# Padded heads straight from the projection for the first 512 tokens of a transformer block

## The chip, the cores and the metric

The kernel runs on one core of one Trainium2 chip. The core has five engines, each with its own instruction queue: TensorE (PE: matrix products from operands in SBUF, results into PSUM), VectorE (DVE), ScalarE (ACT), GpSimd (POOL) and SyncE (SP, which here issues every DMA). Engines run side by side and wait for one another on semaphores. Activations and weights lie in DRAM and are brought into SBUF, the on-chip memory with 128 partitions, by DMA.

The metric is the device time of one execution in microseconds, the median of the runs shown.

## The reference

One transformer block on 2048 tokens of width 640. A vector `c` gives six modulation vectors; a LayerNorm with scale and shift feeds sliding-window attention (32 heads of 20, each query sees itself and the 255 tokens before it), its output is projected, gated and added; a second LayerNorm feeds a gated MLP of width 1536, again gated and added.

```python
mod = (silu(c) @ w_mod).reshape(1, 6, 1, 640)
sa, ca, ga, sb, cb, gb = mod[:, 0..5]
h = layernorm(x) * (1 + ca) + sa
q, k, v = split(h @ wqkv)                      # 32 heads of 20
scores = q @ k.T * 20**-0.5                    # masked: 0 <= i - j < 256
x = x + ga * (softmax(scores) @ v) @ wo
h = layernorm(x) * (1 + cb) + sb
x = x + gb * ((sigmoid(h @ w_gate) * (h @ w_up)) @ w_down)
```

All inputs are bfloat16.

## The kernel before, in words

**Blocks, chunks and parts.** Tokens come in 16 blocks of 128. LayerNorm and the projections work on four chunks of four blocks (512 tokens). Attention, output projection and MLP work on five parts of 2, 2, 4, 4 and 4 blocks (`CHUNKS`, line 363). A part needs keys of its own blocks and of the two blocks before it, so the first two parts need chunk 0 alone, and the third (blocks 4 to 7) needs chunks 0 and 1.

**Order of the work.** The program lists operations with their reads and writes, an engine (or a choice of two), a planned duration, a priority and sometimes an earliest time (`tmin`). `schedule` (line 141) places them greedily: at each step it takes the engine whose next operation can start first, and among that engine's operations that can start at about the same time the one with the lowest priority number. The result is one fixed order for each engine, with buffers given out in that order; `emit` (line 274) writes it with semaphores. On the chip each engine works through its list in order and waits at each entry until its inputs are there, whatever lies behind it. That holds for SP too: a DMA whose source is not ready holds all DMAs behind it. Each DMA also waits for the one 24 places before it (`NDMA`).

**Opening.** `x` of chunk 0, a third of `w_mod` and the Q, K and V weights are loaded. GpSimd fills ten V buffers with ones (line 450) and two `Tn` buffers with zeros. PE runs warm-up matmuls on a V buffer (lines 500 to 509) until `w_mod` is there, and then the products for scale and shift (`scA`, `shA`, lines 568 and 570). `ln_stats` (line 574) computes mean and variance on VectorE and the reciprocal root on GpSimd for all four blocks of a chunk at once, then normalizes block by block (line 594). Chunk 0 is transposed on PE (line 629) and scaled on ScalarE or VectorE (line 634) into `hT`; later chunks are transposed by DMA (line 600).

**Q and K.** A score matmul needs head j of a group of four at partitions 32j to 32j+19, so heads of 20 have to be spread out to a stride of 32. `proj_qk` (line 654) makes five tiles of 128 features for Q and five for K, each a chain of five matmuls of 512 columns (line 513), copies each from PSUM into `stg` (line 648), stores it to DRAM (`dq`, `dk`), and reads it back into `QT` and `KT` by heads (line 674, four reads for each half of the heads). V needs no such round trip: `proj_v` (line 681) puts 20 columns of each head into a stride of 22, beside two columns of ones, which give the sums for the softmax.

**Attention.** For each group of four heads and each set of up to 512 key-query columns: scores on PE (four row tiles of the array at once, line 514), an exponential on ScalarE (line 755), masks on GpSimd (lines 771 and 773), the product with V on PE (line 514), and for each group transposes and the division on VectorE (`norm`, line 819). There is one PSUM buffer for scores. Parts 0 and 1 have 8 and 16 sets, the others 24 each. The result goes through DRAM (`doc`) to be transposed for the output projection. 

**MLP.** `outproj` (line 844) adds, normalizes and transposes into `h2T` (one buffer); `mlp` (line 868) makes gate and up (`wg`, `wu`, resident), tanh on ScalarE, the product on VectorE, and the down projection. PE takes scores (priority 10) and products with V (11) before projections (12 to 23), and the MLP last (40 and up), so projections and MLP fill the time in which scores wait for exponentials.

Of the kernel before, what the change touches and what calls it, by code (L numbers as in the profile page):

```python
# [344 lines left out]
def c_act(n):  # L345
    return 0.17 + n / 1200.0
# [19 lines left out]
def build(nc, A_x, A_wqkv, A_wo, B_x, B_w_gate, B_w_up, B_w_down, c, w_mod, out, S=2048):  # L366
# [17 lines left out]
    wg = sb("wg", [128, NDT, FF])  # L384
    wu = sb("wu", [128, NDT, FF])
# [14 lines left out]
    p_h2 = sbpool("h2T", 1, [128, NDT, 512])  # L400
# [18 lines left out]
    def R(name):  # L419
        return Res(name)  # L420

    R_wq, R_wk, R_wv, R_ident, R_ccol, R_cth, R_siluc, R_silubc = (
        R(n) for n in ("wq", "wk", "wv", "ident", "ccol", "cth", "siluc", "silubc"))
    R_wo = R("wo")
    R_wg = [R(f"wg{t}") for t in range(NDT)]
    R_wu = [R(f"wu{t}") for t in range(NDT)]
# [22 lines left out]
    for i in range(len(p_V.aps)):  # L449
        p_V.init[i].append(A("pool", lambda e, g, i=i: e.memset(p_V.aps[i][:], 1.0), 0.8, writes=[R("vi")], prio=1))  # L450
    for i in range(len(p_Tn.aps)):
        p_Tn.init[i].append(A("pool", lambda e, g, i=i: e.memset(p_Tn.aps[i][:], 0.0), 0.6, writes=[R("ti")], prio=2))
# [27 lines left out]
    for kt in range(NDT):  # L480
        dma(lambda kt=kt: wg[:, kt, :], lambda kt=kt: B_w_gate.rearrange("(t p) f -> p t f", p=128)[:, kt, :], 393216,
            writes=[R_wg[kt]], prio=30, tmin=27 + 1.6 * kt, tag="wg")
        dma(lambda kt=kt: wu[:, kt, :], lambda kt=kt: B_w_up.rearrange("(t p) f -> p t f", p=128)[:, kt, :], 393216,
            writes=[R_wu[kt]], prio=30, tmin=35 + 1.6 * kt, tag="wu")
    for q in range(4):
        dma(lambda q=q: wd[:, 3 * q:3 * q + 3, :],
            lambda q=q: B_w_down.rearrange("(t p) f -> p t f", p=128)[:, 3 * q:3 * q + 3, :], 491520,
            writes=[R_wd[q]], prio=30, tmin=43 + 2.0 * q, tag="wd")
# [17 lines left out]
    for i in range(9):  # L506
        o = A("pe", warm, 0.85, prio=90, extra=p_V.init[0] + wprev, tag="warm", writes=[R("w")])
        wprev = [o]
    p_S.init[0].extend(wprev)

# [63 lines left out]
    def ln_stats(blocks, src, dst, prio):  # L574
# [18 lines left out]
        for bi in range(n):  # L593
            A("dve", lambda e, g, bi=bi: e.tensor_scalar(dst[bi].ap[:], src[bi].ap[:], v(48 + 2 * bi, 1), v(60 + bi, 1),  # L594
                                                         op0=ALU.subtract, op1=ALU.mult), 0.56,
              reads=[src[bi].r(), st.r("r"), st.r(("m", bi))], writes=[dst[bi].r()], prio=prio - 0.5, tag="xh")
# [15 lines left out]
    def ln1(cc):  # L612
# [5 lines left out]
        ln_stats(blocks, src, src, 3 if cc == 0 else 16)  # L618
# [35 lines left out]
    def proj_qk(cc, mts, halves, prio):  # L654
        for which, (w, Rw) in enumerate(((wq, R_wq), (wk, R_wk))):
# [4 lines left out]
            for mt in mts:  # L660
                ps = Tile(p_M, f"{key}{cc}_{mt}")
                pairs = [(lambda kt=kt, mt=mt, w=w, ps=ps: (ps.ap[:], w[:, kt, mt * 128:(mt + 1) * 128],
                                                            hT[cc].ap[:, kt, :])) for kt in range(NDT)]
                s = Tile(p_stg, f"stg{key}{cc}_{mt}")
                pe_chain(ps, 512, pairs, [[Rw, hT[cc].r(kt)] for kt in range(NDT)], prio, f"proj{key}{cc}", hold=[s])
# [12 lines left out]

    dq = {}

    def proj_v(cc, prio):
        for bi in range(4):
            b = 4 * cc + bi
# [30 lines left out]
    def attention(a, i0, QB):  # L714
# [9 lines left out]
        for g in range(NG):  # L724
# [6 lines left out]
            for si, st in enumerate(sets):  # L731
# [17 lines left out]
                for (kb, q0, n) in st:  # L749
                    for j in range(4):  # L750
                        rd[KT[(kb // 4, hh)].r(j)] = 1
                        rd[qt.r(j)] = 1
# [115 lines left out]
    def mlp(a, i0, QB, x1, h2):  # L868
# [4 lines left out]
        for ft in range(NFT):  # L873
            pg, pu, sg = Tile(p_M, "g"), Tile(p_M, "u"), Tile(p_sig, "sig")
            for ps, w, Rw, tg in ((pg, wg, R_wg, "g"), (pu, wu, R_wu, "u")):
                pairs = [(lambda kt=kt, ft=ft, ps=ps, w=w: (ps.ap[:, 0:W], w[:, kt, ft * 128:(ft + 1) * 128],
                                                            h2.ap[:, kt, 0:W])) for kt in range(NDT)]
                last["m"] = [pe_chain(ps, W, pairs, [[Rw[kt], h2.r(kt)] for kt in range(NDT)], pr, f"mlp{tg}{a}",
                                      after=last["m"])]
# [30 lines left out]
    qkv(0)  # L910
    ln1(1)
# [71 lines left out]
```

## Time and profile before

| | us |
|---|---|
| median of 3 runs | 380.7 (377.94 to 381.37) |
| the profiled execution | 380.11 |
| its span, first to last instruction | 378.4 |
| mean granted TensorE clock | 0.954 of full speed |
| PE busy | 344.5 |
| ScalarE busy | 223.0 |
| VectorE busy | 218.8 |
| GpSimd busy | 177.0 |
| moved by DMA | 42.81 MB |

The profile is of one execution. Its times are microseconds from the start of the span, single instructions in nanoseconds where that is said. A row of the timeline gives start, duration, engine, line, operation, what is written and read, how many instructions are merged, and in brackets how long the engine had been idle and what ended that. A row of a group gives busy time, the mean nanoseconds of one instruction, and the idle time ahead of the group by what ended it. "SPq" is SP's queue at work on issuing a DMA; "PEclk" is the clock granted to TensorE as a share of full speed.

### The profile page before, as it was taken

Reading aid. Unit: us, or ns where it says so; the run is one execution under the profiler, and the core shown is the slowest. Engines: PE = TensorE matmul, PEld = TensorE weight load, DVE = VectorE, ACT = ScalarE, POOL = GpSimd, SP = SyncE. Lnnn points to the kernel's source line nnn. Section 1 sums busy time; section 2 is a strip of 40 time slices with the busy share of each in tenths; the row PEclk is TensorE's granted clock in tenths of the full one; section 3 lists DMA queues with packets and bytes.
Section 4 is the critical chain, followed back from the end, with each engine's and each line's share of the span. In section 5 each row is a group of like instructions: output and inputs, shape, how many; then the busy total and the mean of one; then the engine's idle time right before and its main releaser. Section 6 shows DMA issues by size and latency. Waiting matters only on the chain.

```text
span 378.4 us, 8381 instructions
## 1 busy us (share of the span) xinstructions
PE 344.5 (91%) x3198; PEld 172.9 (46%) x3198; DVE 218.8 (58%) x471; ACT 223.0 (59%) x207; POOL 177.0 (47%) x281
## 2 busy tenths in 40 slices
PE   5796697678999799999999879999999999989996
PEld 2453243123445244655556423353554345744464
DVE  4354175767877755556886545397564638433332
ACT  1352366776888769878888767878778421012210
POOL 8111144679676845666668574667567300000000
PEclk9999699579999889999999969999999999999999
DMA  6999799976365042034203511200343020320001
GB/s 215 338 303 192 232 309 373 291 195 197 95 149 144 17 126 75 29 94 101 89 19 88 112 47 36 88 2 20 45 114 87 2 87 3 74 66 0 0 19 52
DMA packets 52887, 42.81 MB, mean 113 GB/s; under 512 B 22768, under 2 KB 49648, under 8 KB 52848
## 3 DMA queue, kind: packets, MB, share of 16 engines
q1 hardware_dynamic: 52848, 42.29, 41.0%
q8 instruction: 25, 0.41, 0.4%
q14 instruction: 14, 0.11, 0.1%
HBM read 27.20 MB, written 10.49 MB: 100 GB/s over the span
## 4 chain that ended last, share of the span: by engine, by line
PE 70%; DMA 8%; POOL 5%; ACT 5%; SPq 5%; issue 3%; DVE 2%; POOLq 0%
PE M L513 57%; PE S L514 7%; PE O L514 6%; SPq L435 5%; ACT E L755 4%; DMA KT<-dk 3%; POOL E L771 3%; DMA wo<-in_A_wo_dram 2%; DMA big<-in_w_mod_dram 1%; POOL E L773 1%; DMA oT<-doc 1%; DVE h2T L605 1%; POOL wo L920 0%; POOL wd L929 0%; DVE x L594 0%
## 5 line engine op out<-in xcount | busy, mean ns | idle before, releaser
L755 ACT ACTIVATE E<-S 128x2048 bf16<-128x2048 f32 (+1 forms) x96 | 169.8, 1769 | 39.5 <-PE S L514 37.0
L771 POOL TENSOR_SCALAR_AFFINE_SELECT E<-E 128x512 bf16<-128x512 bf16 x128 | 83.7, 665 | 99.8 <-ACT E L755 88.2
L773 POOL TENSOR_SCALAR_AFFINE_SELECT E<-E 128x512 bf16<-128x512 bf16 x112 | 72.9, 662 | 0.0
L882 DVE SCALAR_TENSOR_TENSOR big<-sig,M 128x512 bf16<-128x512 f32 (+1 forms) x60 | 34.6, 576 | 62.1 <-PE M L513 53.1
L513 PE MATMUL M<-h2T,wg 128*128 128x512 bf16 (+1 forms) x300 | 64.3, 341 | 1.9 <-DVE h2T L605 1.9
L880 ACT ACTIVATE sig<-M 128x512 f32<-128x512 f32 (+1 forms) x60 | 30.2, 512 | 59.0 <-PE M L513 58.8
L513 PE MATMUL M<-h2T,wu 128*128 128x512 bf16 (+1 forms) x300 | 63.7, 341 | 0.0
L513 PE MATMUL M<-wd,big 128*128 128x320 bf16 x384 | 55.7, 299 | 0.0
L514 PE MATMUL S<-QT,KT 20*128 20x128 bf16 (+2 forms) x768 | 39.0, 280 | 16.2 <-ACT E L755 11.7
L513 PEld LDWEIGHTS M<-wd,big 128*128 128x128 bf16 x384 | 36.4, 98 | 16.9 <-issue 3.0
L514 PE MATMUL O<-E,V 128*32 128x128 bf16 (+2 forms) x768 | 39.0, 282 | 1.7 <-DVE T L822 0.9
L513 PEld LDWEIGHTS M<-h2T,wg 128*128 128x128 bf16 x300 | 28.0, 98 | 26.4 <-issue 3.2
L513 PEld LDWEIGHTS M<-h2T,wu 128*128 128x128 bf16 x300 | 27.7, 99 | 25.3 <-issue 5.2
L514 PEld LDWEIGHTS S<-QT,KT 20*128 20x128 bf16 x768 | 11.7, 94 | 50.0 <-ACT E L755 34.8
L822 DVE STREAM_TRANSPOSE T<-O 128x512 f32<-128x512 f32 x32 | 22.9, 714 | 15.9 <-PE O L514 15.6
L513 PE MATMUL M<-hT,wq 128*128 128x512 bf16 x100 | 29.1, 433 | 2.2 <-DMA dk<-stg 1.6
L648 ACT ACTIVATE stg<-M 128x512 bf16<-128x512 f32 x28 | 16.7, 598 | 23.2 <-PE M L513 21.7
L892 DVE TENSOR_TENSOR x<-M,x 128x320 bf16<-128x320 f32 x32 | 15.7, 489 | 24.8 <-PE M L513 24.8
L583 DVE BATCH_NORM_STATS2 st<-x 128x6 f32<-128x320 bf16 x64 | 27.2, 473 | 3.9 <-DMA x<-in_A_x_dram 3.7
L513 PE MATMUL M<-wv,hT 128*128 128x320 bf16 x160 | 26.1, 306 | 1.1 <-DVE hT L605 1.1
L513 PE MATMUL M<-hT,wk 128*128 128x512 bf16 x100 | 25.7, 392 | 0.4 <-DMA dq<-stg 0.4
L513 PE MATMUL M<-wo,oT 128*128 128x320 bf16 x160 | 24.5, 300 | 1.1 <-DMA oT<-doc 1.1
(50 smaller groups left out, 255.5 us busy)
## 6 DMA issues: line engine op xcount, KB each, us to landing
x<-in_A_x_dram SPq DMA_DIRECT2D x32, 160.0 KB
big<-in_w_mod_dram SPq DMA_DIRECT2D x15, 320.0 KB
dq<-stg SPq DMA_DIRECT2D x20, 128.0 KB
dk<-stg SPq DMA_DIRECT2D x20, 128.0 KB
QT<-dq SPq DMA_DIRECT2D x32, 80.0 KB
KT<-dk SPq DMA_DIRECT2D x32, 80.0 KB
doc<-On SPq DMA_DIRECT2D x64, 40.0 KB
out_dram<-x SPq DMA_DIRECT2D x16, 160.0 KB
```

The source lines that it names most:

```text
L435: return e.dma_start(dst(), src())
L513: return e.matmul(o, l, r, start=st, stop=sp, skip_group_check=True)
L514: return e.matmul(o, l, r, start=st, stop=sp, tile_position=tp, skip_group_check=True)
L583: ins = e.bn_stats(v(bi * 12 + j * 6, 6), src[bi].ap[:, j * 320:(j + 1) * 320])
L648: return e.activation(dst(), src(), ACT.Copy)
L755: A("act", lambda e, eng, E=E, Sp=Sp, ncol=ncol: e.activation(E.ap[:, :, 0:ncol], Sp.ap[:, :, 0:ncol], ACT.Exp, scale=SM_SCALE), c_act(4 * ...
L771: return e.affine_select(ap, ap, pattern=[[0, 4], [1, 128]], compare_op=ALU.is_ge, fill=0.0, base=0, channel_multiplier=-1)
L773: return e.affine_select(ap, ap, pattern=[[0, 4], [-1, 128]], compare_op=ALU.is_ge, fill=0.0, base=-1, channel_multiplier=1)
L822: A("dve", lambda e, g: e.transpose(T1.ap[:], O.ap[:]), c_dve(512), reads=[O.r()], writes=[T1.r()], prio=4, tag="tr1")
L880: A("act", lambda e, g, pg=pg, sg=sg: e.activation(sg.ap[:, 0:W], pg.ap[:, 0:W], ACT.Tanh, scale=0.5), c_act(W), reads=[pg.r()], writes=[s ...
L882: A("dve", lambda e, g, pu=pu, sg=sg, ft=ft: e.scalar_tensor_tensor(out=hv(ft), in0=sg.ap[:, 0:W], scalar=1.0, in1=pu.ap[:, 0:W], op0=ALU. ...
L892: A("dve", lambda e, g, ps=ps, bi=bi, half=half: e.tensor_tensor(x1[bi].ap[:, half * 320:half * 320 + 320], ps.ap[:, 0:320], x1[bi].ap[:, ...
```

## The change

1. **Q and K of chunk 0 without DRAM.** The weights of Q and K are copied on chip into a padded form, 32 columns for each head of 20 with zeros between. A product with these puts each head where the score matmul wants it, and one PSUM copy writes it into `QT` or `KT` (`proj_qk_direct`). A tile of 128 padded columns is one group of four heads, so there are eight chains for each of Q and K. Chunks 1 to 3 go through DRAM as before. Scores of chunk 0 wait for one group's tile and no longer for a half's four reads.
2. **Where the padded weights lie.** Gate and up weights become one buffer, and the padded weights use it first. The ten loads of gate and up can be issued once the last padded product has been planned, with an earliest time of 32 in the plan.
3. **Loads and LayerNorm in halves.** Q and K weights are loaded in two halves of 320 columns each, with V's between. Chunk 0's LayerNorm runs as two calls of two blocks, with its own priorities.
4. **Opening.** V buffers get ones only where ones are used; the `Tn` fills come earlier; warm-up matmuls use a `Tn` buffer, 24 of one matmul instead of 9 of two.
5. **`h2T` has two buffers.** Blocks 2 and 3 of V get priority 12.95, between the padded groups.

```diff
-    wg = sb("wg", [128, NDT, FF])
-    wu = sb("wu", [128, NDT, FF])
+    p_wgu = Pool("wgu", [sb("wgu", [128, 2, NDT, FF])])
...
-    p_h2 = sbpool("h2T", 1, [128, NDT, 512])
+    p_h2 = sbpool("h2T", 2, [128, NDT, 512])
...
-        p_V.init[i].append(A("pool", lambda e, g, i=i: e.memset(p_V.aps[i][:], 1.0), 0.8, writes=[R("vi")], prio=1))
+        p_V.init[i].append(A("pool", lambda e, g, i=i: e.memset(
+            p_V.aps[i][:, 0:H * VW].rearrange("p (h j) -> p h j", j=VW)[:, :, DH:VW], 1.0), 0.2, writes=[R("vi")],
+            prio=3))
+        p_V.init[i].append(A("pool", lambda e, g, i=i: e.memset(p_V.aps[i][:, H * VW:H * VW + 10], 1.0), 0.1,
+                             writes=[R("vi")], prio=3))
...
-    dma(lambda: wq[:], lambda: wqkv_src[:, :, 0:D], 819200, writes=[R_wq], prio=0.3, tag="wq")
-    dma(lambda: wk[:], lambda: wqkv_src[:, :, D:2 * D], 819200, writes=[R_wk], prio=0.31, tag="wk")
+    for half in range(2):
+        for k_, (w, Rw) in enumerate(((wq, R_wq), (wk, R_wk))):
+            dma(lambda w=w, half=half: w[:, :, half * 320:half * 320 + 320],
+                lambda k_=k_, half=half: wqkv_src[:, :, k_ * D + half * 320:k_ * D + half * 320 + 320], 409600,
+                writes=[Rw[half]], prio=0.3 + 0.1 * half + 0.01 * k_, tag="wqk")
...
+    wpad = Tile(p_wgu, "wpad")
+
+    def wp_ap(which):
+        return wpad.ap[:, which, :, :].rearrange("p t f -> p (t f)")[:, 0:NDT * 1024].rearrange(
+            "p (t f) -> p t f", t=NDT)
+    for which, (w, Rw) in enumerate(((wq, R_wq), (wk, R_wk))):
+        A("pool", lambda e, g, which=which: e.memset(
+            wp_ap(which).rearrange("p t (h j) -> p (t h) j", j=32)[:, :, DH:32], 0.0), 1.9,
+          writes=[wpad.r((which, "z"))], prio=0.6, tag="wpz")
+    for half in range(2):
+        for which, (w, Rw) in enumerate(((wq, R_wq), (wk, R_wk))):
+            for k0, k1 in ((0, 2), (2, 4), (4, 5)):
+                def cp(e, g, which=which, k0=k0, k1=k1, w=w, half=half):
+                    d = wp_ap(which)[:, k0:k1, half * 512:half * 512 + 512].rearrange(
+                        "p t (h j) -> p t h j", j=32)[:, :, :, 0:DH]
+                    r = w[:, k0:k1, half * 320:half * 320 + 320].rearrange("p t (h j) -> p t h j", j=DH)
+                    if g == "act":
+                        return e.activation(d, r, ACT.Copy)
+                    return e.tensor_copy(d, r)
+                n = 320 * (k1 - k0)
+                A(("act", "pool"), cp, {"act": c_act(n), "pool": c_pool(n)}, reads=[Rw[half], wpad.r((which, "z"))],
+                  writes=[wpad.r((which, half, k0 // 2))], prio=2 + half, tag="wpad")
...
-        for k in range(2):
-            ins = e.matmul(p_S.aps[0][:, 0, :], p_V.aps[0][:, 0:128], p_V.aps[0][:, 0:512], start=True, stop=True)
+        for k in range(1):
+            ins = e.matmul(p_S.aps[0][:, 0, :], p_Tn.aps[0][:, 0:128], p_Tn.aps[0][:], start=True, stop=True)
...
-        ln_stats(blocks, src, src, 3 if cc == 0 else 16)
+        if cc == 0:
+            ln_stats(blocks[:2], src[:2], src[:2], 0.5, 0.7)
+            ln_stats(blocks[2:], src[2:], src[2:], 0.5, 0.7)
+        else:
+            ln_stats(blocks, src, src, 16)
...
+    def proj_qk_direct(prio):
+        for hh in range(2):
+            for which in range(2):
+                (QT, KT)[which][(0, hh)] = Tile((p_QT, p_KT)[which], f"{'qk'[which]}T0_{hh}")
+            for gl in range(4):
+                for which in range(2):
+                    t = (QT, KT)[which][(0, hh)]
+                    ps = Tile(p_M, f"d{which}_{hh}_{gl}")
+                    c0 = (4 * hh + gl) * 128
+                    pairs = [(lambda kt=kt, which=which, ps=ps, c0=c0: (
+                        ps.ap[:], wp_ap(which)[:, kt, c0:c0 + 128], hT[0].ap[:, kt, :])) for kt in range(NDT)]
+                    pe_chain(ps, 512, pairs, [[wpad.r((which, hh, kt // 2)), hT[0].r(kt)] for kt in range(NDT)],
+                             prio + (2 * (4 * hh + gl)) * 0.1, "projd", hold=[t])
+                    evac(lambda t=t, gl=gl: t.ap[:, gl, :], lambda ps=ps: ps.ap[:], 512, [ps.r()], [t.r(("g", gl))], 2,
+                         "evd")
...
-            proj_qk(0, (0, 1, 2), (0,), 12)
-            proj_v(0, 13)
-            proj_qk(0, (3, 4), (1,), 14)
+            proj_qk_direct(12)
+            proj_v(0, 12.35)
...
+    wgu = Tile(p_wgu, "wgu")
+    for w, src in enumerate((B_w_gate, B_w_up)):
+        for kt in range(NDT):
+            dma(lambda kt=kt, w=w: wgu.ap[:, w, kt, :],
+                lambda kt=kt, src=src: src.rearrange("(t p) f -> p t f", p=128)[:, kt, :], 393216,
+                writes=[wgu.r((w, kt))], prio=28, tmin=32.0, tag="wg")
```

More of the change, by code (lines that the diff above doesn't have):

```diff
@@ L420, in R @@
         return Res(name)
[L422 to L423 removed]
+    R_wq, R_wk = [R("wq0"), R("wq1")], [R("wk0"), R("wk1")]
+    R_wv, R_ident, R_ccol, R_cth, R_siluc, R_silubc = (
+        R(n) for n in ("wv", "ident", "ccol", "cth", "siluc", "silubc"))
     R_wo = R("wo")
[L425 to L426 removed]
     R_wd = [R(f"wd{t}") for t in range(4)]
@@ L571, in build, with ln_stats @@
       reads=[psA.r(), R_mA], writes=[R_mA], prio=0)
-    def ln_stats(blocks, src, dst, prio):
+    def ln_stats(blocks, src, dst, prio, xprio=None):
         n = len(blocks)
@@ L664, in proj_qk @@
                 s = Tile(p_stg, f"stg{key}{cc}_{mt}")
-                pe_chain(ps, 512, pairs, [[Rw, hT[cc].r(kt)] for kt in range(NDT)], prio, f"proj{key}{cc}", hold=[s])
+                pe_chain(ps, 512, pairs, [Rw + [hT[cc].r(kt)] for kt in range(NDT)], prio, f"proj{key}{cc}", hold=[s])
                 evac(lambda s=s: s.ap[:], lambda ps=ps: ps.ap[:], 512, [ps.r()], [s.r()], 6, "evqk")
@@ L682, in proj_v @@
         for bi in range(4):
+            if cc == 0 and bi == 2:
+                prio = 12.95
             b = 4 * cc + bi
@@ L749, in attention @@
                 for (kb, q0, n) in st:
-                    for j in range(4):
-                        rd[KT[(kb // 4, hh)].r(j)] = 1
-                        rd[qt.r(j)] = 1
+                    for tl in (KT[(kb // 4, hh)], qt):
+                        for key in ([("g", gl)] if ("g", gl) in tl.res else range(4)):
+                            rd[tl.r(key)] = 1
                 last["s"] = [A("pe", sc, ncol / 2400.0 + 0.02, reads=list(rd), writes=[Sp.r()], prio=10, lat=0.25,
```

22 lines of the change are left out of this document (9 added, 13 removed).

## The prediction

> **What bounds the kernel now.** I read the head of the page first, then its chain of waits by engine, to see which engine the end hangs on.
>
> ```profile
> span 378.4 us, 8381 instructions
> PE 344.5 (91%) x3198; PEld 172.9 (46%) x3198; DVE 218.8 (58%) x471; ACT 223.0 (59%) x207; POOL 177.0 (47%) x281
> ...
> PE 70%; DMA 8%; POOL 5%; ACT 5%; SPq 5%; issue 3%; DVE 2%; POOLq 0%
> ```
>
> PE is busy for 91% of the span and makes 70% of the chain, and no other engine is above 59%. So to a first approximation the time is PE's work plus what PE loses by standing idle or by running at a lower clock. An average hides where the loss lies, so the next view is the table of windows, cut where the trace changes character (stretch, its length, busy time of each engine with its count, granted clock, DMA share, GB/s).
>
> ```profile
> core 0: us, PE busy (x) PEld busy (x) DVE busy (x) ACT busy (x) POOL busy (x), PEclk, DMA share, GB/s
> 15.90:28.00 12.10, 12.10 (x70) 6.67 (x71) 5.66 (x17) 7.21 (x14) 1.27 (x2) 1.00 0.89 294
> 28.00:41.20 13.20, 7.07 (x56) 3.67 (x54) 4.72 (x12) 2.23 (x4) 1.40 (x1) 0.96 0.99 197
> 41.20:50.00 8.80, 8.79 (x59) 3.61 (x60) 2.97 (x6) 4.56 (x5) 2.46 (x4) 0.67 0.92 247
> 50.00:70.00 20.00, 15.16 (x185) 7.70 (x183) 13.22 (x30) 12.77 (x15) 9.47 (x14) 0.94 1.05 364
> 70.00:85.00 15.00, 10.98 (x123) 3.09 (x119) 11.54 (x21) 11.13 (x10) 10.69 (x14) 0.63 1.02 207
> 85.00:104.70 19.70, 18.22 (x218) 8.04 (x214) 15.54 (x38) 15.21 (x15) 15.72 (x23) 1.00 0.51 145
> 104.70:200.00 95.30, 92.22 (x1020) 49.56 (x1016) 64.43 (x140) 77.90 (x67) 62.09 (x101) 0.96 0.33 85
> 200.00:294.60 94.60, 90.37 (x929) 41.60 (x932) 57.53 (x117) 74.04 (x55) 60.55 (x98) 0.96 0.26 62
> 294.60:378.40 83.80, 79.78 (x479) 43.52 (x474) 35.77 (x72) 14.92 (x23) 3.81 (x7) 1.00 0.12 34
> ```
>
> I multiply PE's busy time by its granted clock and call it full-clock work. The first six rows give 12.10 + 6.79 + 5.89 + 14.25 + 6.92 + 18.22 = 64.2 us of work in 88.8 us, or 0.72. The last three give 0.93, 0.92 and 0.95. So the stage from 15.9 to 104.7 us loses 24.6 us, about as much as the 274 us behind it together (18.6 us). The loss lies in the four rows between 28 and 85 us. The timeline says why.
>
> ```profile
> 12.56 0.16 DVE L570 TENSOR_SCALAR shA<-M 128x5 f32<-128x5 f32 x1
> 12.63 1.15 DVE L594 TENSOR_SCALAR x<-x,st 128x640 bf16<-128x640 bf16 x3
> ...
> 14.27 2.31 ACT L634 ACTIVATE hT<-M,shA,scA 128x512 bf16<-128x512 f32 x3 [10.36 <-PE M L513]
> ...
> 15.87 3.52 PE L513 MATMUL M<-hT,wq 128*128 128x512 bf16 x15
> ...
> 21.38 2.32 PE L513 MATMUL M<-hT,wk 128*128 128x512 bf16 x10
> ...
> 23.81 1.24 PE L513 MATMUL M<-hT,wk 128*128 128x512 bf16 x5
> ...
> 27.64 7.63 SPq L600 DMA_TRANSPOSE hT<-x  x4
> ...
> 36.06 1.44 SPq L435 DMA_DIRECT2D KT<-dk  x4
> ...
> 41.22 0.51 PE L514 MATMUL S<-QT,KT 20*128 20x256 bf16 x8 [2.95 <-DMA KT<-dk]
> ...
> 58.84 6.35 SPq L435 DMA_DIRECT2D wd<-in_B_w_down_dram  x3
> ```
>
> K's first three projection tiles are computed by 25.05 us (23.81 + 1.24), but their reads back from DRAM are issued only at 36.06, behind four transposing DMAs that hold SP's queue for 7.63 us, and the first score matmul runs at 41.22, after 2.95 us of waiting on that read. That is 25.3 us from the first projection (15.87) to the first score. In between PE runs out of independent work: 6.1 us idle between 28 and 41.2.
>
> **The change, part by part.** *Q and K of the first 512 tokens.* Ten chains of five matmuls (five tiles each for Q and K) become sixteen (eight head groups each), because a padded group holds 80 useful columns in 128. That is 30 more matmuls with 512 moving columns. Ten of them took 2.32 us and five 1.24, so five more cost 1.08 us, 0.216 us each, and 30 cost 6.5 us. All of it lands on PE, which sets the end: **+6.5 us**. What goes in exchange are the ten stores to DRAM and the sixteen reads back (four for each of two halves of Q and K), with their places in SP's queue: the four KT reads held it for 1.44 us. What stands between projection and score is now one PSUM copy. The first score needs only group 0 of Q and of K, two chains (2.2 us) and a copy of 0.6 us, so it moves from 41.22 to about 19 us, and all 24 score sets of the first two attention parts need no key or query beyond these 512 tokens. From then on PE has projections to fill the time in which ScalarE computes exponentials.
>
> How much of the 24.6 us comes back? The work of the stage becomes 64.2 + 6.5 = 70.7 us. With 0.72 it would take 97.8 us, with the rate of the first row (1.00) 70.7 us; these are the ends. Nearest is a stage in which attention and projections already interleave with their inputs at hand: the row from 85 to 104.7 gives 18.22/19.70 = 0.925, and the two long rows behind it 0.93 and 0.92. I take 0.92: 70.7/0.92 = 76.8 us, against 88.8 now. **Net −12.0 us**, the added matmuls included.
>
> One rule speaks on the clock in this. The rows at 41.2 to 50 (0.67, behind the 2.95 us gap) and at 70 to 85 (0.63) lose 2.9 and 4.1 us of work between them. In the second stretch the gaps are short:
>
> ```profile
> PE S L514 <- ACT E L755: 11.7, 10, 1.8
> ```
>
> That is PE's waits of scores on exponentials: 11.7 us in ten waits, none over 1.8 us, so here the clock fell without a long gap. The Trainium skill (TensorE: Matmul & The Clock Gate, "HAM oscillation — how this bites in real kernels") tells the reader to avoid PE-idle gaps over about 3.4 us. Read strictly, the rule lowers the clock for a long gap alone, so filling many short ones would not restore the 4.1 us, and its sum would be 371.5 us of this execution instead of the 367.4 below. The rows just shown speak against that reading.
>
> *Padding the weights on chip.* Twelve strided copies on ScalarE or GpSimd and two zero fills on GpSimd are new. ScalarE's nearest rows are its PSUM copies:
>
> ```profile
> L648 ACT ACTIVATE stg<-M 128x512 bf16<-128x512 f32 x28 | 16.7, 598 | 23.2 <-PE M L513 21.7 <-DVE wo L920 1.2
> ...
> L648 ACT ACTIVATE V<-M 128x320 bf16<-128x320 f32 x18 | 7.9, 437 | 4.5 <-PE M L513 4.3
> ```
>
> From 320 to 512 columns is 0.161 us, 0.84 ns a column, so a copy of 640 costs 0.705 us, and each half of Q's or K's weights (640, 640, 320) 1.85 us: 7.4 us for all four if ScalarE did everything. GpSimd's rows that can stand for a copy are these:
>
> ```profile
> L771 POOL TENSOR_SCALAR_AFFINE_SELECT E<-E 128x512 bf16<-128x512 bf16 x128 | 83.7, 665 | 99.8 <-ACT E L755 88.2 <-PE M L513 11.4
> ...
> L450 POOL MEMSET V<- 128x714 bf16 x10 | 6.4, 695 | 0.0
> L929 POOL TENSOR_TENSOR wd<-wd,gbc 128x640 bf16<-128x640 bf16 x3 | 4.4, 1467 | 0.0
> ```
>
> A 640-column copy lies between 0.83 us (1.3 ns a column, the mask) and 1.47 us (the product); I take 1.0, nearer to the mask, which also reads one tensor. The zero fills cover 1920 columns each, 1.9 us at the fill's 0.97 ns, 3.7 us together. The ten full V fills (6.4 us) shrink to 20 of 64 or 10 columns, a tenth of the columns, so GpSimd's opening work grows only if each costs over 0.13 us ((6.4 − 3.7)/20). The first half of both weights, 3.7 us of copies, takes about 2 us on two engines and is hidden as far as the weights land while hT is still being made. If GpSimd took 1.47 us and had to do most, the first K chain would wait some 2 us more: the bad end. The second half is needed 8 chains (8.6 us) later and is hidden.
>
> *LayerNorm in halves.* The last normalized block is ready at 13.78 (12.63 + 1.15) and the first scaling of hT starts at 14.27. In halves the second pair no longer waits for four blocks' statistics, but the scaling also needs shA, ready at 12.72. So 1.5 us can be won at most, and then the padded weights are next. I take **−0.7 us**, between −1.5 and +2.0.
>
> *The rest.* Six more PSUM copies (16 for 10) are 3.6 us of ScalarE or VectorE, both under 60% busy. wq and wk in halves are two more issues on SP. Warm-up from another tile has no user. Two h2T buffers let the next part's LayerNorm run ahead of the MLP; I cost that at nothing, since the late rows are at 0.92 and more with one. **A new wait:** gate and up weights now share storage with the padded weights, so their ten loads wait for the last padded chain. Queued behind them on SP are the stores and reads of the next tokens' Q and K and attention's stores. I cost it at nothing: the cover is that MLP, as now, uses those weights only after the first attention part and its output projection, and that the planner puts the loads where it expects the release. If PE runs later than planned, SP stands by that much, and rival 3 prices it.
>
> **The sum.** 380.1 (the profiled execution: span 378.4 and 1.7 around it) − 12.0 − 0.7 = 367.4 us. The median of the runs is 0.6 above that execution, so **368 us**.
>
> **The rivals.**
> 1. *The clock stays low.* While exponentials pace the scores, PE gets 0.63 as it does from 70 to 85 us, however its short gaps are filled: the 4.1 us of that row are not won, 367.4 + 4.1 + 0.6 = 372 us. For it: one score set still waits for the exponential ahead of it. Against it: the row from 85 to 104.7 has the same waits and 1.00. Chance 0.12. (The strict reading of the Trainium skill's rule, above, would come out here.)
> 2. *The starvation moves.* Tokens 512 to 1023 still go through DRAM, their transposes start no earlier than their x arrives, and the third attention part needs them. If the first two parts end early and PE then waits, the stage lands midway at 0.82: 86.2 us, a gain of 2.6, 377 us. For it: 27.64 to 36.06 was SP at work for these tokens. Against it: the gate and up weights can fill. Chance 0.17.
> 3. *Slower: SP blocks on the release of the padded weights.* Three loads of wd that held SP for 6.35 us at 58.84 stand just ahead of the worst row. Ten loads that wait for PE hold back the next Q and K in the same way. If the stage stays at 0.72 it takes 97.8 us and, with 0.7 won ahead, the time is 380.1 + 9.0 − 0.7 + 0.6 = 389. It turns from gain to loss once the stage loses over 18.8 us (88.8 + 0.7 − 70.7). Against it: the wait is as long as PE's lag behind its plan, and that must be over ten us. Chance 0.09.
>
> **How the numbers follow.** Forecast 0.62, spread 358 to 375: the full rate of 1.00 gives 70.7 us in the stage and, with 1.5 won ahead, 361, and a few us may come from the later stages when MLP work is at hand earlier; 0.87 gives 81.3 us, 372, or 375 with the bad end of the copies. One per cent, about what a measurement of this kernel tells from no change, is 3.8 us, so faster means under 376.9. Faster takes the forecast, rival 1 and 0.05 of rival 2: 0.79. Same is the rest of rival 2: 0.12. Slower is rival 3: 0.09. The range 358 to 379 leaves out rival 3 and some 0.08 at the ends.
>
> **What would show it.** In the changed profile the first score should start near 19 us and wait on a PSUM copy, not on a DMA; the stage up to the first score of the third part should have PE at 0.9 or more; Q and K's first chains should start between 14 and 18 us. Scores waiting on DMA, a stretch of SP before the gate weights' loads longer than 5 us, or a clock near 0.6 before 80 us would show rivals 2, 3 and 1. I am wrong if the first score comes early and the end does not move: then the late rows have lost what the early ones won.

## The result, and the profile after

The changed kernel takes **361.96 us** (median of 4 runs, 360.86 to 364.79), the kernel before beside it 379.32 us (375.33 to 381.37). The ratio is 0.9587, with a 95% interval of 0.9478 to 0.9696. The forecast was 368, range 358 to 379.

Here is the head of the page of the changed kernel. The profiled execution is the slowest of the four, 364.79 us.

```profile
span 363.0 us, 8445 instructions
PE 342.2 (94%) x3234; PEld 174.5 (48%) x3234; DVE 229.2 (63%) x477; ACT 224.7 (62%) x210; POOL 183.4 (51%) x304
```

PE's busy time barely changes (344.5 before), although it has more to do. The span around it is shorter. The table of windows, cut this time at the first score of the third attention part (84.7 us) and around a hole that was not there before, shows where (columns as in the prediction):

```profile
15.90:84.70 68.80, 63.60 (x652) 29.65 (x651) 49.62 (x111) 51.54 (x58) 39.35 (x59) 1.00 0.88 265
84.70:104.70 20.00, 20.00 (x213) 9.40 (x213) 14.70 (x32) 16.45 (x15) 12.19 (x20) 1.00 0.66 154
104.70:110.00 5.30, 5.20 (x76) 2.98 (x72) 5.20 (x13) 4.02 (x4) 4.81 (x9) 1.00 0.27 74
110.00:125.00 15.00, 8.99 (x92) 3.75 (x93) 14.11 (x24) 9.70 (x7) 13.57 (x18) 0.88 0.27 71
125.00:150.00 25.00, 22.98 (x231) 11.30 (x229) 16.21 (x27) 18.57 (x17) 14.88 (x20) 0.93 0.23 68
150.00:280.00 130.00, 129.43 (x1421) 67.27 (x1420) 84.68 (x178) 106.23 (x84) 86.85 (x140) 1.00 0.26 65
280.00:363.00 83.00, 80.24 (x464) 44.16 (x462) 35.95 (x72) 13.41 (x23) 1.27 (x2) 1.00 0.12 34
```

The first row is at 63.60/68.80 = 0.92 and at full clock. Between 28 and 85 us the kernel before lost 23 of 57 us. After 150 us PE is nearly full. In between there is a new loss: PE works 9 of 15 us from 110 to 125, while VectorE (14.11) and GpSimd (13.57) are nearly full, and the clock then falls. In a median run, 2.8 us shorter than this one, the hole may be smaller.

The timeline of the opening, answering to the one shown of the kernel before:

```profile
12.34 1.10 ACT L509 ACTIVATE wgu<-wq 128x640 bf16<-128x640 bf16 x2 [8.45 <-DMA wq<-in_A_wqkv_dram]
...
13.51 1.11 POOL L510 COPY wgu<-wk 128x640 bf16<-128x640 bf16 x2 [0.37 <-DMA wk<-in_A_wqkv_dram]
...
14.94 3.54 PE L537 MATMUL M<-hT,wgu 128*128 128x512 bf16 x15
...
18.40 0.12 PEld L538 LDWEIGHTS S<-QT,KT 20*128 20x128 bf16 x8 [0.42 <-DVE KT L677]
18.41 0.34 PE L538 MATMUL S<-QT,KT 20*128 20x256 bf16 x8
```

The padded copies of the first half end at 14.62 (13.51 + 1.11), just ahead of the first padded chain. The first score runs at 18.41, 22.8 us earlier than before, and what released it is a PSUM copy.

### The profile page after: what moved, and what is told of

It reads as the page before. It is cut to its first block, busy times and chain, and to the rows that moved or that the text cites. A ratio compares the mean times of both kernels' runs of the same rounds, so it can differ in the third digit from the quotient of the medians.

```text
span 363.0 us, 8445 instructions
## 1 busy us (share of the span) xinstructions
PE 342.2 (94%) x3234; PEld 174.5 (48%) x3234; DVE 229.2 (63%) x477; ACT 224.7 (62%) x210; POOL 183.4 (51%) x304
## 4 chain that ended last, share of the span: by engine, by line
PE 68%; DVE 5%; ACT 3%; DMA 2%; issue 2%; SPq 2%; POOL 1%; DVEq 0%; POOLq 0%
PE M L537 56%; PE S L538 6%; PE O L538 6%; ACT E L801 3%; DMA dk<-stg 2%; DVE h2T L629 2%; SPq L433 2%; DVE hT L629 1%; POOL E L819 0%; DVE Tn L872 0%; POOL wo L971 0%; DVE On L877 0%; DVE stg L677 0%; POOL E L817 0%; DVE wo L971 0%
## 5 line engine op out<-in xcount | busy, mean ns | idle before, releaser
L537 PE MATMUL M<-h2T,wgu 128*128 128x512 bf16 (+1 forms) x600 | 112.4, 338 | 1.1 <-DVE h2T L629 1.1
L537 PEld LDWEIGHTS M<-h2T,wgu 128*128 128x128 bf16 x600 | 56.1, 98 | 49.9 <-issue 5.4
L538 PE MATMUL S<-QT,KT 20*128 20x128 bf16 (+2 forms) x768 | 37.1, 267 | 5.9 <-ACT E L801 5.5
L538 PE MATMUL O<-E,V 128*32 128x128 bf16 (+2 forms) x768 | 37.5, 272 | 0.6 <-POOL E L819 0.6
L868 DVE STREAM_TRANSPOSE T<-O 128x512 f32<-128x512 f32 x32 | 22.8, 714 | 17.7 <-PE O L538 17.3
L537 PE MATMUL M<-wv,hT 128*128 128x320 bf16 x160 | 25.2, 300 | 0.0
L537 PE MATMUL M<-hT,wq 128*128 128x512 bf16 x75 | 20.5, 410 | 3.8 <-DVE hT L629 1.7
L877 DVE STREAM_TRANSPOSE On<-Tn 128x512 bf16<-128x512 bf16 x32 | 22.6, 706 | 0.7
L538 PEld LDWEIGHTS O<-E,V 128*32 128x32 bf16 x768 | 11.7, 94 | 21.6 <-issue 13.7
L537 PE MATMUL M<-hT,wk 128*128 128x512 bf16 x75 | 18.5, 380 | 2.5 <-DMA dq<-stg 1.7
L618 DVE TENSOR_SCALAR x<-x,st 128x640 bf16<-128x640 bf16 x32 | 17.6, 580 | 3.3 <-POOL st L615 3.3
```

What stands on the lines that cost most here:

```text
L537: return e.matmul(o, l, r, start=st, stop=sp, skip_group_check=True)
L538: return e.matmul(o, l, r, start=st, stop=sp, tile_position=tp, skip_group_check=True)
L868: A("dve", lambda e, g: e.transpose(T1.ap[:], O.ap[:]), c_dve(512), reads=[O.r()], writes=[T1.r()], prio=4, tag="tr1")
L877: A("dve", lambda e, g: e.transpose(On.ap[:, half * 512:half * 512 + 512], Tn.ap[:]), c_dve(512), reads=[Tn.r()], writes=[On.r(half)], pri ...
```

## The experiments

All times are medians; each ratio is to the kernel before, run on the same chip beside it. The kernel before took 377.35 to 379.88 us beside the experiments and 379.32 beside the change, so a difference of two rows in microseconds carries some 2 us from that. Where a difference is small, I also give the difference of the ratios, times 379.32 us. No experiment leaves any of the computation out.

| kernel | us | ratio to before, 95% interval |
|---|---|---|
| the change | 361.96 | 0.9587, 0.9478 to 0.9696 |
| all but the padded projection | 374.65 | 0.9875, 0.9805 to 0.9945 |
| padded projection only | 373.89 | 0.9856, 0.9801 to 0.9911 |
| padded projection, short fills, new warm-up | 363.51 | 0.9621, 0.9542 to 0.9700 |
| change with full fills | 367.74 | 0.9755, 0.9685 to 0.9824 |
| change with scores planned late | 369.53 | 0.9777, 0.9694 to 0.9860 |
| change with 32 more matmuls | 366.23 | 0.9647, 0.9587 to 0.9706 |
| change with one h2T buffer | 365.11 | 0.9641, 0.9575 to 0.9706 |
| change with whole LayerNorm | 361.19 | 0.9527, 0.9465 to 0.9589 |
| change with another earliest time | 363.70 | 0.9604, 0.9529 to 0.9678 |
| change with both modulation products early | 366.15 | 0.9666, 0.9595 to 0.9736 |
| change with the third part's products early | 355.94 | 0.9432, 0.9370 to 0.9495 |
| change with wd scaled on VectorE | 357.54 | 0.9434, 0.9374 to 0.9495 |

**All but the padded projection.** The fills and copies of the padded weights go as well (cut here).

```diff
...
-            proj_qk_direct(12)
-            proj_v(0, 12.35)
+            proj_qk(0, (0, 1, 2), (0,), 12)
+            proj_v(0, 13)
+            proj_qk(0, (3, 4), (1,), 14)
```

> Everything of the change but the padded projection: Q and K of the first 512 tokens go through DRAM again and no weights are padded. Theory A (the gain is the early stage that fills up because scores start near 18 us): first score near 40 us again, PE under 0.8 between 28 and 85 us, 374 to 382 us. Rival B (the gain comes from the small parts, two h2T buffers, halves, less SP traffic later): 362 to 367 us.

374.65 us. Its PE timeline waits on the same read as the kernel before:

```profile
41.35 0.35 PE L515 MATMUL S<-QT,KT 20*128 20x256 bf16 x8 [1.85 <-DMA KT<-dk]
```

The early stage is as starved as it was, as theory A says. The small parts alone bring 1.2%, so rival B has a share, a small one.

**The padded projection only.** One h2T buffer, LayerNorm of chunk 0 whole, fills and warm-up as before.

```diff
-    p_h2 = sbpool("h2T", 2, [128, NDT, 512])
+    p_h2 = sbpool("h2T", 1, [128, NDT, 512])
...
+        p_V.init[i].append(A("pool", lambda e, g, i=i: e.memset(p_V.aps[i][:], 1.0), 0.8, writes=[R("vi")], prio=1))
...
-            ins = e.matmul(p_S.aps[0][:, 0, :], p_Tn.aps[0][:, 0:128], p_Tn.aps[0][:], start=True, stop=True)
+            ins = e.matmul(p_S.aps[0][:, 0, :], p_V.aps[0][:, 0:128], p_V.aps[0][:, 0:512], start=True, stop=True)
...
-        if cc == 0:
-            ln_stats(blocks[:2], src[:2], src[:2], 0.5, 0.7)
-            ln_stats(blocks[2:], src[2:], src[2:], 0.5, 0.7)
-        else:
-            ln_stats(blocks, src, src, 16)
+        ln_stats(blocks, src, src, 3 if cc == 0 else 16)
```

> The padded projection with its weight loads in halves and its shared buffer, but LayerNorm of the first chunk whole, warm-up and fills as before, one h2T buffer. Theory A: first score near 20 us, 361 to 367 us. Rival B: 372 to 380 us, since the parts that it credits are gone.

373.89 us: outside theory A's range and inside rival B's. Neither half of the change has much of the gain alone. The timeline of this kernel says what went wrong:

```profile
1.72 3.34 POOL L494 MEMSET wgu<- 128x1920 bf16 x2
...
4.99 6.41 POOL L448 MEMSET V<- 128x714 bf16 x10
...
12.03 1.05 POOL L610 TENSOR_TENSOR st<-st,mhalf 128x4 f32<-128x4 f32 x1
...
16.98 1.09 ACT L505 ACTIVATE wgu<-wq 128x640 bf16<-128x640 bf16 x2 [1.16 <-DMA wq<-in_A_wqkv_dram]
...
19.06 1.43 ACT L653 ACTIVATE hT<-M,shA,scA 128x512 bf16<-128x512 f32 x2
...
26.26 0.34 PE L533 MATMUL S<-QT,KT 20*128 20x256 bf16 x8
```

The zero fills and the full fills of ones hold GpSimd until 11.4 us, so LayerNorm's root ends at 13.08 (9.78 in the changed kernel). Transposition slips, and then ScalarE, in its fixed order, waits 1.16 us, until 16.98, for the second half of Q's weights, with two pieces of hT queued behind its copies. hT is complete at 21.3 us (15.8 in the changed kernel), and the first score runs at 26.26. The late start also costs clock: PE works only 1.67 us from 15 to 20 us, the granted clock from 20 to 25 us is 0.50, and the first fifteen padded matmuls take 6.05 us instead of 3.54. So the shortened fills, or the new warm-up, seemed to be needed. The next two runs test the fills alone, and fills and warm-up together with the padded projection.

**Full fills, all else as changed.**

```diff
-        p_V.init[i].append(A("pool", lambda e, g, i=i: e.memset(
-            p_V.aps[i][:, 0:H * VW].rearrange("p (h j) -> p h j", j=VW)[:, :, DH:VW], 1.0), 0.2, writes=[R("vi")],
-            prio=3))
-        p_V.init[i].append(A("pool", lambda e, g, i=i: e.memset(p_V.aps[i][:, H * VW:H * VW + 10], 1.0), 0.1,
-                             writes=[R("vi")], prio=3))
+        p_V.init[i].append(A("pool", lambda e, g, i=i: e.memset(p_V.aps[i][:], 1.0), 0.8, writes=[R("vi")], prio=1))
```

> The changed kernel, but the ten V buffers are filled with ones in full again (at their old priority), 6.4 us of GpSimd in place of 2.5. Theory F (the padded projection needs a short GpSimd opening: with the old fills and the new zero fills GpSimd reaches LayerNorm's root 3 us late and what is planned behind it slips, as in the kernel with the padded projection alone, where the first score runs at 26.3 us): first score 2 to 8 us later than 18.4, 366 to 373 us. Rival (the fills are off the path, the forecast's reading): 361 to 364 us.

367.74 us, 5.8 more than the change; first score:

```profile
24.58 0.34 PE L534 MATMUL S<-QT,KT 20*128 20x256 bf16 x8
```

Theory F holds: one line of fills moves the first score by 6.2 us and the end by 5.8 (6.4 by the ratios). The edit changes both the length of the fills and their priority, so it does not say which of the two matters. Here too the clock is low when the padded chains start (0.54 from 15 to 20 us, 0.77 from 20 to 25), although the new warm-up is in place.

**Padded projection with short fills and new warm-up,** without the second h2T buffer and without halves in LayerNorm.

```diff
-    p_h2 = sbpool("h2T", 2, [128, NDT, 512])
+    p_h2 = sbpool("h2T", 1, [128, NDT, 512])
...
-        if cc == 0:
-            ln_stats(blocks[:2], src[:2], src[:2], 0.5, 0.7)
-            ln_stats(blocks[2:], src[2:], src[2:], 0.5, 0.7)
-        else:
-            ln_stats(blocks, src, src, 16)
+        ln_stats(blocks, src, src, 3 if cc == 0 else 16)
```

> The changed kernel without the second h2T buffer and without the LayerNorm in halves: padded projection, short fills and new warm-up alone. Theory F: the pair is what makes the gain, 361 to 366 us. If it needs the two other parts as well: 368 us or more.

363.51 us: padded projection, fills and warm-up have nearly all of the gain. The warm-up was never taken out alone, so its own share is not shown.

**Scores planned late.** The padded projection stays; the score operations get an earliest time.

```diff
-                               tag=f"score{a}", extra=last["s"], mode=1)]
+                               tag=f"score{a}", extra=last["s"], mode=1, tmin=40.0)]
```

> The changed kernel, padded projection and all, but no score is planned before 40 us, about when the first ran in the kernel before. Theory A (what counts is that scores start early, so that PE has them to interleave): PE runs the 16 padded chains and V until about 40 us without a gap, then the 24 early score sets pace it with less to fill them: 5 to 10 us lost, 367 to 372 us. Rival E (what counts is that the DRAM trip with its DMAs is gone; the scores' date does not matter): 360 to 364 us.

369.53 us, 7.6 more than the change (7.2 by the ratios), in theory A's range. PE has no gap up to the first score in its timeline, and yet time is lost:

```profile
37.66 0.59 PE L537 MATMUL M<-hT,wgu 128*128 128x512 bf16 x2
38.09 3.40 PE L537 MATMUL M<-hT,wq 128*128 128x512 bf16 x15
41.43 0.34 PE L538 MATMUL S<-QT,KT 20*128 20x256 bf16 x8
```

PE has used up the chains that should have lain between scores: from 41.2 to 104.7 us it does 53.4 us of full-clock work, in the change 58.3. So the date of the first score counts by itself. It is not all: with its first score at 41.43 us this kernel is still 5.1 us faster than the one without the padded projection (374.65, first score at 41.35; 3.7 us by the ratios), whose PE is busy for 7.95 us from 28 to 41.2 us, where here it works through padded chains for 13.15.

**32 more matmuls.** The first matmul of each padded chain is issued three times.

```diff
+                    for _ in range(dup if k == 0 else 0):
+                        mm(e, o, l, r, True, True)
...
-                             prio + (2 * (4 * hh + gl)) * 0.1, "projd", hold=[t])
+                             prio + (2 * (4 * hh + gl)) * 0.1, "projd", hold=[t], dup=2)
```

> The changed kernel with each of the 16 padded chains' first matmul issued three times (32 matmuls of 512 columns more, planned as such, result the same). If PE work in this stage counts in full (the forecast's +6.5 us for 30): 32 x 0.216 = 6.9 us more, 369 us. If the stage had slack on PE that hides it: 362 to 364 us.

366.23 us, 4.3 more by the medians and 2.3 by the ratios, between the two expectations. In this kernel's profile the hole behind the stage is smaller (104.7 to 150 us: 41.04 us of PE against 37.17), so some of the added work seems to have filled time that the change loses there. That is a reading of one profile and no proof.

**One h2T buffer.**

```diff
-    p_h2 = sbpool("h2T", 2, [128, NDT, 512])
+    p_h2 = sbpool("h2T", 1, [128, NDT, 512])
```

> The changed kernel with one h2T buffer. Forecast (the second buffer is worth nothing): 360 to 364 us. Rival B (it lets LayerNorm run ahead of the MLP and gives the late gain): 366 us or more.

365.11 us, 3.2 more than the change (2.0 by the ratios), between the two ranges; the intervals overlap. The windows from 200 to 280 us are clearer. First the change, then this kernel:

```profile
200.00:280.00 80.00, 79.81 (x826) 37.52 (x824) 49.09 (x100) 63.93 (x47) 52.30 (x84) 1.00 0.23 57
```

```profile
200.00:280.00 80.00, 76.21 (x756) 34.39 (x763) 51.80 (x102) 59.77 (x42) 48.07 (x79) 0.98 0.24 62
```

With two buffers PE does 79.8 us of full-clock work here, with one 74.7 (76.21 × 0.98). The kernel with short fills and one buffer has 74.3. In the kernel without the padded projection, which has two buffers, it is only 75.4 (76.97 × 0.98), so the size depends on the rest of the order. I take the buffer to be worth some 5 us of this stage in the changed kernel; how much of it reaches the end these runs leave between 0 and 5.

**LayerNorm whole.**

```diff
-        if cc == 0:
-            ln_stats(blocks[:2], src[:2], src[:2], 0.5, 0.7)
-            ln_stats(blocks[2:], src[2:], src[2:], 0.5, 0.7)
-        else:
-            ln_stats(blocks, src, src, 16)
+        ln_stats(blocks, src, src, 3 if cc == 0 else 16)
```

> The changed kernel with the first chunk's LayerNorm in one call of four blocks at its old priority. Forecast (halves are worth 0.7 us, at most 1.5): 362 to 364 us, hT about 1 us later. If the halves matter more, 365 us or more.

361.19 us, no slower than the change. The first score comes at 19.51, 1.1 us later, and the end does not follow. Even that 1.1 us can't be put down to the halves: in the next run, which keeps them, the first score comes at 19.56. The halves are worth nothing that shows here.

**Another earliest time** for the gate and up loads.

```diff
-                writes=[wgu.r((w, kt))], prio=28, tmin=32.0, tag="wg")
+                writes=[wgu.r((w, kt))], prio=28, tmin=46.0, tag="wg")
```

> The changed kernel with the gate and up weights' earliest planned time 46 instead of 32, a change with no work in it; it shows how far the planner's reshuffling alone moves the time. No effect: 360 to 364 us. If the order is worth microseconds by itself, outside that.

363.70 us, inside the expectation: 1.7 us more by the medians, 0.6 by the ratios, with overlapping intervals. Reordering by the planner alone may move the time by that much, and I read nothing into less than 2 us. The profile moves more: this kernel's PE is idle for 9.7 us from 104.7 to 150, the change's for 8.1.

**The hole at 110 to 125 us.** In the changed kernel PE is so full early on that the products for the modulation's second and third part, at priorities 30 and 31, are reached at 59 to 63 and at 106 to 109 us. The scaling of `wd`, which needs the third, then falls where the first MLPs' `h2T` must be scaled. VectorE's and GpSimd's timelines of the changed kernel:

```profile
109.95 3.77 DVE L629 TENSOR_SCALAR h2T<-h2T,scB,shB 128x256 bf16<-128x256 bf16 x5
```

```profile
110.50 1.39 POOL L980 TENSOR_TENSOR wd<-wd,gbc 128x640 bf16<-128x640 bf16 x1
111.84 0.63 POOL L817 TENSOR_SCALAR_AFFINE_SELECT E<-E 128x512 bf16<-128x512 bf16 x1
112.43 1.21 POOL L819 TENSOR_SCALAR_AFFINE_SELECT E<-E 128x512 bf16<-128x512 bf16 x2
```

Five scalings take 3.77 us; the first five took 2.08 in the kernel before:

```profile
112.30 2.08 DVE L605 TENSOR_SCALAR h2T<-h2T,scB,shB 128x256 bf16<-128x256 bf16 x5
```

What PE itself waits for from 104 to 130 us of the changed kernel (in total, times, longest):

```profile
PE S L538 <- ACT E L801: 3.2, 3, 1.6
PE M L537 <- DVE hT L629: 1.7, 1, 1.7
PE M L537 <- DVE h2T L629: 1.1, 1, 1.1
```

So 2.8 us are waits for VectorE's scalings, and 3.2 us are scores that wait for exponentials while PE's order holds no other work. I tried both products early, then the third part alone:

```diff
-    mod_bc(wmB, 0, 0.5, 30)
+    mod_bc(wmB, 0, 0.5, 11.8)
...
-    mod_bc(wmC, 640, 0.25, 31)
+    mod_bc(wmC, 640, 0.25, 11.9)
```

(and `mod_cols` beside each in the same way.)

> The changed kernel with the products of the second and third part of the modulation weights at priority 11.8 and 11.9 instead of 30 and 31, so ahead of the projections. In the changed kernel these come at 59 to 63 and 106 to 109 us, and the scaling of wd by gbc falls at 110 to 125 us, where PE stands idle for 6 of 15 us while VectorE's h2T scaling takes 0.8 us a piece beside GpSimd's wd products. Theory C (the late products cause that hole): the hole goes, 350 to 357 us. Rival D (VectorE and GpSimd are short of time there with or without wd): the hole stays or moves, 360 to 364 us.

366.15 us, slower than the change and outside both expectations. The hole closes (43.97 us of PE in 45.3 from 104.7 to 150), and another opens, where PE stands in its order before a load of the third part:

```profile
45.01 0.40 PE L537 MATMUL M<-silubc,big 128*128 128x100 bf16 x5 [3.08 <-DMA big<-in_w_mod_dram]
```

With only the third part moved:

```diff
-    mod_bc(wmC, 640, 0.25, 31)
+    mod_bc(wmC, 640, 0.25, 21.5)
...
-    cC = mod_cols(wmC, 0, psC, 31)
+    cC = mod_cols(wmC, 0, psC, 21.5)
```

> The changed kernel with only the products of the third part of the modulation weights moved up (priority 21.5 instead of 31, ahead of the third chunk's projections, behind the second's); the second part's stay at 30, so that PE does not stand in front of a load that has not landed, as it did from 41 to 50 us when both were moved up. Theory C: wd is scaled before 110 us, the hole at 110 to 125 us closes by 4 us or more and no other opens, 355 to 359 us. Rival D (VectorE is short of time there anyway): 360 to 364 us.

**355.94 us**, 354.95 to 357.12 in four runs, all below the fastest run of the change. Its windows:

```profile
104.70:150.00 45.30, 43.29 (x481) 22.07 (x481) 33.01 (x66) 37.79 (x35) 34.44 (x51) 1.00 0.37 86
150.00:280.00 130.00, 129.34 (x1356) 65.15 (x1356) 82.93 (x175) 101.95 (x80) 82.46 (x132) 1.00 0.25 62
```

From 104.7 to 150 us PE does 43.3 us of full-clock work instead of 34.2 (37.17 × 0.92), as theory C says. It also expected `wd` to be scaled before 110 us, and that is not so for all of it: two of GpSimd's seven products start at 116.3 and 120.2 us. This is the fastest kernel of the study.

The last run asks whether it is the date alone:

```diff
-        A(("pool", "dve"), lambda e, g, t=t: e.tensor_tensor(wd[:, t, :], wd[:, t, :], gbc[:], op=ALU.mult), WS,
+        A(("dve",), lambda e, g, t=t: e.tensor_tensor(wd[:, t, :], wd[:, t, :], gbc[:], op=ALU.mult), WS,
```

> The changed kernel with all twelve wd products on VectorE; in the changed kernel GpSimd does five of them, 1.48 us each, and VectorE's ten h2T scalings of 256 columns take 0.81 us each (0.50 in the kernel before). Theory G (GpSimd's long products hold VectorE back in the hole at 110 to 125 us): the scalings fall to about 0.5 us, PE's idle time from 105 to 151 us from 8.1 to 5 us or less, 357 to 360 us. Theory C alone (the products come at the wrong time, whoever does them): five more products of 0.5 to 0.9 us on VectorE, hole as long or longer, 361 to 366 us.

357.54 us. The groups of `h2T` scalings and of `wd` products on VectorE, of the change and of this kernel:

```profile
L629 DVE TENSOR_SCALAR h2T<-h2T,scB,shB 128x256 bf16<-128x256 bf16 x10 | 7.5, 813 | 0.0
L980 DVE TENSOR_TENSOR wd<-wd,gbc 128x640 bf16<-128x640 bf16 x7 | 6.4, 933 | 0.0
```

```profile
L980 DVE TENSOR_TENSOR wd<-wd,gbc 128x640 bf16<-128x640 bf16 x12 | 8.1, 695 | 0.1
L629 DVE TENSOR_SCALAR h2T<-h2T,scB,shB 128x256 bf16<-128x256 bf16 x10 | 3.6, 427 | 0.0
```

Without GpSimd's products the mean scaling takes 0.43 us instead of 0.81, and VectorE, with five products more, does all twelve in 8.1 us where it needed 6.4 for seven. The means mix cases. Here is one scaling of the changed kernel beside a product of GpSimd, and one beside a mask:

```profile
110.50 1.39 POOL L980 TENSOR_TENSOR wd<-wd,gbc 128x640 bf16<-128x640 bf16 x1
110.52 1.44 DVE L629 TENSOR_SCALAR h2T<-h2T,scB,shB 128x256 bf16<-128x256 bf16 x1
...
112.43 0.63 POOL L819 TENSOR_SCALAR_AFFINE_SELECT E<-E 128x512 bf16<-128x512 bf16 x1
112.47 0.67 DVE L629 TENSOR_SCALAR h2T<-h2T,scB,shB 128x256 bf16<-128x256 bf16 x1
```

Each lasts about as long as GpSimd's instruction. In the changed kernel two of the ten scalings lie beside a product and eight beside masks. In this kernel three lie beside masks, and the other seven take about 0.33 us. So the masks hold VectorE back as well, and part of the gain in the mean is that fewer scalings happen to meet them here. The Trainium skill (SBUF — State Buffer, "SBUF: two separate sides") says that some VectorE operations and GpSimd share one pair of SBUF ports, held for a whole instruction while the other blocks; these numbers agree with it.

PE's idle time from 104.7 to 150 falls from 8.1 to 3.6 us. From 104 to 130 us its waits for VectorE are gone, and those for exponentials stay:

```profile
PE S L538 <- ACT E L801: 3.0, 3, 1.7
```

Theory G holds for the waits on VectorE. That it is the cause of the whole hole is not shown: with whole LayerNorm GpSimd still does five products there and the scalings take 0.68 us in the mean, yet PE is idle for only 3.7 us, at a clock of 1.00.

## Why the prediction was right, and where not

**The stage from 15.9 us on.** Right, and nearly to the microsecond. The change does 63.6 us of full-clock work up to 84.7 and needs 7.1 more to reach the forecast's 70.7; at the full rate of the next row it has them at 91.8. That is 75.9 us against a forecast of 76.8, with 0.92 as the rate up to the third part's first score. The first score at 18.41 ("about 19") waits on a PSUM copy, as forecast.

**The clock, and rival 1.** The first two rows after are at 1.00, so it came back with the gaps filled, and rival 1 falls. The prediction's row of waits on exponentials (11.7 us in ten) counts the whole span; from 70 to 85 us there are three, 4.0 us in all, none over 1.8, so its point stands. The strict reading of the Trainium skill's rule falls too (TensorE: Matmul & The Clock Gate, "HAM oscillation — how this bites in real kernels"): in the new hole the clock falls to 0.65 and 0.67 in the two windows of 5 us from 120 on, with no single gap of PE over 1.73 us from 110 to 125:

```profile
110.00:115.00 5.00, 2.27 (x32) 1.28 (x36) 5.00 (x10) 3.79 (x3) 4.66 (x7) 1.00 0.38 76
115.00:120.00 5.00, 3.45 (x47) 1.32 (x49) 5.00 (x7) 4.03 (x3) 5.00 (x6) 1.00 0.39 117
120.00:125.00 5.00, 3.27 (x23) 1.16 (x16) 4.11 (x9) 1.88 (x1) 3.91 (x7) 0.65 0.06 19
125.00:130.00 5.00, 5.00 (x47) 2.06 (x48) 3.01 (x6) 2.86 (x3) 1.15 (x2) 0.67 0.24 81
```

Over the span the clock is a large part of the gain: the kernel before loses 17.4 us to it (378.4 × 0.046), the change 3.3 (363.0 × 0.009), though some of that falls on time in which PE was idle.

**+6.5 us for 30 matmuls.** Not confirmed in full: 32 more cost 4.3 us by the medians, 2.3 by the ratios, where 6.9 were forecast. Where the rest goes is not shown; the smaller hole behind the stage is a candidate.

**The opening.** The step that failed is the fills, which I weighed only by GpSimd's total. "Warm-up from another tile has no user" belongs to it, but no run tests the warm-up alone. The total was right: zero fills 3.3 us and short fills 2.5 replace 6.4. But the fills, by their length or their place, decide whether the padded projection starts at 15 or near 20 us, 5.8 us of the end. I had said what would be late if the copies were slow, and not what would be late if the fills were not shortened. A copy on GpSimd cost less than both ends of its range:

```profile
L510 POOL COPY wgu<-wq 128x640 bf16<-128x640 bf16 x2 | 1.4, 718 | 4.4 <-DMA wq<-in_A_wqkv_dram 4.4
```

That is 0.72 us against 0.83 to 1.47; the fills are the nearer row (0.97 ns a column gives 0.62), not the masks. ScalarE's copy took 0.74 against 0.705.

**LayerNorm in halves, −0.7 us.** Not shown. Without halves the first score comes 1.1 us later, but so it does in the run that changes only an earliest time, and the end does not move.

**The second h2T buffer, nothing.** This term was mis-sized. The late rows at 0.92 and more seem to have had its loss in them: from 150 us on the change loses 3.3 of 213 us where the kernel before lost 11.6 of 228.4. The buffer is one part of that; the rest these runs do not divide.

**Rival 3.** SP did not block on the release, by its timeline and PE's:

```profile
41.19 0.82 PE L537 MATMUL M<-hT,wgu 128*128 128x512 bf16 x3
```

```profile
40.36 1.49 SPq L433 DMA_DIRECT2D doc<-On  x4
42.10 2.27 SPq L433 DMA_DIRECT2D wgu<-in_B_w_gate_dram  x5
```

The last padded product ends at 42.01 and the first gate load is issued at 42.10; SP was at work until 41.85.

**Rival 2.** The starvation did move, but not to the place I named. The third part's first score did not wait for keys or queries, though from 50 to 85 us PE lost 3.0 us in four waits on the stores of later tokens' Q and K. The larger hole came 25 us after that score, about half of it for want of VectorE's scalings and half for exponentials. From 104.7 to 150 us the change does 5.2 us less full-clock work than the kernel before.

**The sum.** For the profiled execution 367.4 was forecast and 364.8 measured. The early stage was forecast right; the later rows gave 8.3 us beyond 150 and took 5.2 in the hole, together 3. With the 0.9 of the early stage that is more than the 2.6 measured; clocks of two digits leave this account good to about a microsecond and a half. That a gain and a loss of this size, neither of them forecast, nearly cancel is luck. The rest of the 6 us between 368 and 362 is the median: it lies 2.8 us below the profiled execution, where I had set it 0.6 above.

## What to carry to other kernels

On an engine that sets the time, count its full-clock work stage by stage; an edit that adds work can pay if it makes work available where the engine starves, and the rate of a neighbouring stage whose inputs are at hand is a good guess of what it will reach. When engines run in a fixed order, ask which small operations at the start (fills, copies) stand ahead of the first item of the new path, because such a line can carry a third of the gain (5.8 of 17.4 us here). After such a gain, look for what was only done early because the engine had been idle: here the modulation products slid by 30 to 45 us, onto the first MLPs' scalings, and one priority that moves the third part's products away from there won 6 us more.

## What the runs showed of the hardware that was not expected

- GpSimd copied 640 strided bfloat16 columns in 0.72 us, as fast as ScalarE (0.74 us).
- VectorE's scaling of 256 columns took about 0.33 us alone, 0.67 us beside a mask of GpSimd (0.63 us) and 1.44 us beside a product of GpSimd (1.39 us).
- TensorE's clock was still 1.00 while PE worked 5.7 of the 10 us from 110, and 0.65 in the next 5 us, with no gap over 1.73 us.
